# Relative-bias attention and a snake feed-forward layer on one core: the order of the opening's loads, zero products and bias factors

## The chip, the cores and the metric

One core of one Trainium2 chip. The metric is device time of one execution in microseconds (us). Engines are called PE (TensorE, matrix products), ACT (ScalarE), DVE (VectorE), POOL (GpSimd) and SP (SyncE, which only issues transfers here).

## The reference

Attention over 8 batch entries with 8 heads, 576 positions and 64 columns a head, with a bias that depends on the distance of two positions alone; its output, 4608 rows by 512, goes through a feed-forward layer of width 2048.

```python
scores = scale * np.matmul(q, k.transpose(0, 1, 3, 2))      # scale = 1/8
bucket = ...                                                # of |i - j|, 31 from 116 on
scores = scores + bias_table[bucket].transpose(2, 0, 1)[None]
attn = softmax(scores)
x = np.matmul(attn, v)                                      # -> (8*576, 512)
h = x @ w_in                                                # 512 -> 2048
s = np.sin(alpha * h)
g = h + s * s / (alpha + 1e-09)
out = g @ w_out                                             # 2048 -> 512, float32
```

## The kernel before

Everything is computed in fp16 with fp32 sums. For each batch entry t the kernel makes transposed scores (keys on the 128 partitions, queries along the row), takes their exponential on ACT, multiplies the band near the diagonal by a factor exp(bias - last bias) on DVE, and multiplies by the values with a column of ones beside them, which gives the softmax's sum as well. DVE divides by it (`norm_av`), PE or a transfer turns the result into `xT`, and then come the products with `w_in` (16 blocks f of 128 columns), sine, square, `g`, and the products with `w_out`. After the opening PE works through all this without a gap.

**Planner.** The order of instructions on each engine comes from a list scheduler in the kernel (`Plan`). A task has costs for the engines that may run it, dependencies, a priority `pri` (lower first) and a time `nb` before which it isn't taken. The planner always takes the task with the earliest start; among those within 0.02 us on one engine, the one with the lowest `pri`. The plan's clock is its own; what the engines then do is in that order, and each waits for its operands. A "fill" is a product of zeros (`warm1`) of 192 columns that is put on PE where the plan would leave it free for over `WARM_GAP`, from plan time `WARM_FROM` to `WARM_END`; a task's `pad` lists further zero products that always follow it if a bank of the accumulator is free. A fill holds a bank in the planner's books.

**Opening, t = 0.** SP loads k and then q of heads 0 and 1 (`nat0`), then the values of heads 0 and 1 (`load_v32`, fp32, cast later by POOL). ACT's queue loads the bias table, the constant `phi`, and alpha. POOL loads heads 2 to 5 (`load_pair`), later 6 and 7. DVE casts k, DVE and POOL each one half of q. PE turns k and q of a pair of heads p (`plan_tr`: PE transposes, a copy on DVE, for k also `tail` on POOL, which puts the last 64 keys into `kts`). The bias: PE subtracts the last bucket (`less`), ACT takes exp into `tabE`, PE multiplies it by `phi` (8 partitions x 512), ACT copies that to `e_sb` and writes it in several copies to the scratch tensor `e_dram`; SP waits for that write and then reads from it, with one element's shift for each partition, the band rows `m2r` (heads 0-1, 2-3, 4-7) and `mhr`, rows for the last 64 keys. Behind them SP loads the values of heads 4 to 7.

The scores of t = 0 run unit by unit (`plan_att0`): for each pair p four units "A" of 128 keys (two products of 512 columns, one for each head) and one unit "C" for the last 64 keys. Each unit: PE, then exp on ACT (L704), then the factor product `bd` on DVE (L735 for A; for C L721, on DVE for p = 0 and on POOL for the others). POOL's first load of `w_in` stands behind a one-element copy `tick` from `m2r`, so that it waits for the last band rows; behind it come the loads of k, q of t = 1 and `w_out` (`loads2`) and the values of t = 1 (`loads3`). `clear` sets the zeros and ones in the second set of buffers, which t = 1 needs.

Constants that the change touches: `T_FIRST` (k's and q's first transposes), `T_TAB` (`less`), `T_PAIR` (transposes of pairs 1 to 3), `T_M2`, `T_MH` (factor products), `T_V0`, `T_VA`, `T_VB` (values' loads and casts), `T_WI`, `T_CL`, `T_W`, `T_TR1`, `T_WO` (w_in's loads, clear, first products with w_in, transposes of t = 1, first products with w_out). `T_ACT` lists pairs whose q copy goes to ACT.

Of the kernel before, what the change touches and what calls it, by code (L numbers as in the profile page):

```python
# [10 lines left out]
F16 = mybir.dt.float16  # L11
# [50 lines left out]
class Plan:  # L62
# [86 lines left out]
    def run(self, t0):  # L149
        free = {e: t0 for e in ("PE", "ACT", "DVE", "POOL", "SP")}  # L150
        todo = list(self.tasks)
        while todo:
# [33 lines left out]
            if e == "PE" and WARM_FROM < free[e] < WARM_END and st > free[e] + WARM_GAP:  # L186
                if self.fill(free[e], 192):
                    free[e] += 0.083
                    continue
# [27 lines left out]
PRI_S = 0  # L217
T_WI = 16.8
T_TAB = 5.2
T_CL = 24.5  # L220
T_FIRST = (4.75, 5.95)
T_PAIR = ((7.9, 8.5), (9.3, 10.2), (11.6, 12.3))
T_ACT = ()
T_M2 = (13.0, 14.8, 16.0, 16.0)
T_MH = 14.2
T_RST = 25.0
T_V0 = (5.8, 6.4, 8.9, 9.6)
T_P3 = 7.0
T_VA = (10.5, 11.0)
T_VB = (19.5, 19.5, 19.5, 19.5)  # L230
T_AL = (10.0, 560)
# [7 lines left out]
T_V = ((15.5, 19.0), (50.0, 50.0))  # L239
T_TR1 = (36.0, 39.0)  # L240
T_W = (25.5, 30.5)
T_WO = (40.5, 43.0, 45.7, 48.3)
WARM0 = 8
WARM1 = 2
WARM_LAG = 0.3
WARM_GAP = 0.12
WARM_FROM = 7.3
AV_PRI = 400
# [18 lines left out]
def kernel(  # L267
# [25 lines left out]
    EW = 512  # L293
    NE = 5

# [6 lines left out]
    staged_q = nc.dram_tensor("staged_q", [T, S, H * D], F16, kind="Internal")  # L302
    e_dram = nc.dram_tensor("e_dram", [NE, 4 * H, EW], F16, kind="Internal")

# [76 lines left out]
    def bank(b, n=1):  # L381
        k = b.banks[0]
        return pb[:, k, :] if n == 1 else pb[:, k : k + n, :]
# [31 lines left out]
    def load_v32(h):  # L415
        nc.sync.dma_start(out=vst[:, h], in_=v[0, h, 0:512].rearrange("(c p) d -> p c d", p=128))
# [36 lines left out]
    def full(out, lhsT, rhs, start, stop):  # L453
        nc.tensor.matmul(out=out, lhsT=lhsT, rhs=rhs, start=start, stop=stop)  # L454
# [13 lines left out]
    def load_m2r(eng, h0, h1, r):  # L468

        eng.dma_start(  # L470
            out=m2r[:, h0:h1],
            in_=bass.AP(tensor=e_dram, offset=EW * (4 * H * r + h0), ap=[[1, 128], [EW, h1 - h0], [1, XW]]),
        )

    def load_mhr(eng):
        for z in range(2):
            eng.dma_start(
                out=mhr[64 * z : 64 * z + 64],
                in_=bass.AP(tensor=e_dram, offset=EW * (4 * H * (1 + z) + z) + 192,
                            ap=[[1, 64], [2 * EW, NP], [1, 192]]),  # L480
            )
# [31 lines left out]
    P_.tensor_copy(out=natb[:, 1, :, 1], in_=x0[:, :, 1])  # L513

# [5 lines left out]
    def loads3():  # L520
        load_v16(1)
# [16 lines left out]
    def plan_tr(t, p, kq, pri, nb, deps=()):  # L538
# [45 lines left out]
    def plan_table():  # L584

        a, b = Buf("h"), Buf("h")

        def less(e):
            full(bank(a)[0:NB, 0:H], less_last, tabN, True, True)

        def ex(e):
            nc.scalar.activation(out=tabE, in_=bank(a)[0:NB, 0:H], func=AF.Exp)

        x = plan.add({"PE": 0.06}, less, [], -1200, nb=T_TAB, new=[a])
        x.pad = (256,)
        x = plan.add({"ACT": 0.12}, ex, [x], -1200, use=[a])

        def mm(e):
            full(bank(b)[0:H, 0:EW], tabE, phi_sb, True, True)

        def cp(e):
            nc.scalar.activation(out=e_sb, in_=bank(b)[0:H, 0:EW], func=AF.Copy)
# [52 lines left out]
    def plan_unit(t, p, kind, c, u, ub, done, gate, base):  # L655
# [51 lines left out]
        x = plan.add({"ACT": n / 1200.0 + 0.065}, ex, [mark] + gate, base + 20, use=[b, ub])  # L707
        late = 0.0 if t else T_MH if kind == "C" else T_M2[p]
        if kind == "X":
# [6 lines left out]
        elif kind == "C":  # L716
            ys = slice(0, 2) if two else slice(y, y + 1)

            def bd(e):
                io = u.v[:, ys, 8, 384:512]  # L720
                k_of(e).tensor_tensor(  # L721
                    out=io, in0=io, in1=mh[:, 2 * g + ys.start : 2 * g + ys.stop, 0:128], op=ALU.mult
                )
# [38 lines left out]
    def plan_att0(g, gates, gate):  # L762
# [6 lines left out]
        for i, unit in enumerate(runs):  # L769
# [5 lines left out]
            def run(e, i=i, x=x):  # L775
# [6 lines left out]
                if g == 1 and i == len(runs) - 1:  # L782
# [444 lines left out]
```

## Time and profile before

| | us |
|---|---|
| three runs | 375.42, 375.47, 377.07 |
| median | 375.47 |
| profiled execution, device time | 376.99 |
| its span in the profile | 375.1 |
| PE busy in the span | 367.5 (98%) |
| ACT, DVE, POOL busy | 309.7, 262.3, 92.7 |
| first score product / first exp | 7.91 / 8.45 |
| `e_dram` write issued / SP's first `m2r` load issued | 6.90 / 10.75 |
| first factor product on DVE | 16.17 |
| `tick` on POOL / first `w_in` load issued | 20.18 / 20.69 |
| last exp of t = 0 ends | 28.5 |
| first product with `w_in` | 30.44 |

Times below the fourth row count from the start of the span. Busy times of PE are those of pipelined products, so 98% isn't 98% of its peak. Between the span and the device time lie 1.9 us.

### The profile page before, as it was taken

How to read it: one execution, taken by the hardware profiler on the slowest of the kernel's cores; microseconds unless marked ns; L12 is line 12 of the kernel's file. 1: busy time of each engine (PE TensorE's matmuls, PEld its weight loads, DVE VectorE, ACT ScalarE, POOL GpSimd, SP SyncE). 2: the span in 40 equal slices, each digit the busy share in tenths (PEclk: the TensorE clock that was granted, in tenths of full speed). 3: DMA queues.
4: the chain of work that ended last, by engine and by line, in shares of the span. 5: the costliest groups of instructions: out<-in, count | busy, mean ns of one | idle time of the engine just before them, and what ended most of it. 6: DMA issues, size and time to landing. Idle time of an engine off the chain costs nothing.

```text
span 375.1 us, 8928 instructions
## 1 busy us (share of the span) xinstructions
PE 367.5 (98%) x3576; PEld 196.4 (52%) x3576; DVE 262.3 (70%) x569; ACT 309.7 (83%) x421; POOL 92.7 (25%) x133
## 2 busy tenths in 40 slices
PE   7989999999999999999999999999999999999996
PEld 3465545644464445784564456444666456444443
DVE  3696976778676957696769767886769576879000
ACT  3797989889997979797979799879979797999211
POOL 7477360064000910064004600190006000000000
PEclk9799999999999999999999999999999999999999
DMA  9979999599724992299929992799259121000112
GB/s 167 190 139 206 199 167 147 120 98 122 123 61 97 103 174 73 68 144 137 130 54 140 118 163 58 133 92 172 69 97 121 65 57 48 7 27 5 72 69 85
DMA packets 149114, 40.49 MB, mean 108 GB/s; under 512 B 137080, under 2 KB 143568, under 8 KB 149072
## 3 DMA queue, kind: packets, MB, share of 16 engines
q0 software_dynamic: 96032, 17.67, 58.2%
q1 hardware_dynamic: 52864, 22.16, 24.2%
q8 instruction: 28, 0.46, 0.5%
q10 hardware_dynamic: 176, 0.09, 0.1%
q14 instruction: 14, 0.11, 0.1%
HBM read 37.73 MB, written 16.56 MB: 145 GB/s over the span
## 4 chain that ended last, share of the span: by engine, by line
PE 93%; ACT 4%; DMA 1%; DVE 0%; issue 0%; POOL 0%; SPq 0%; ACTq 0%
PE pb L454 91%; ACT u L704 4%; PE pb L553 1%; DMA natx<-in_q_dram 1%; PE pb L1021 1%; DVE qT L536 0%; POOL natx L513 0%; PE pb L547 0%; DVE xn L950 0%; DVE u L735 0%; SPq L429 0%; ACT outs L534 0%; ACT xT L534 0%; PE pb L643 0%; PE pb L931 0%
## 5 line engine op out<-in xcount | busy, mean ns | idle before, releaser
L704 ACT ACTIVATE u<-pb 128x1024 f16<-128x1024 f32 (+1 forms) x146 | 136.1, 1019 | 18.2 <-PE pb L454 18.0
L454 PE MATMUL pb<-w_out,g 128*128 128x512 f16 (+2 forms) x592 | 138.6, 374 | 0.0
L454 PE MATMUL pb<-xT,w_in 128*128 128x512 f16 (+4 forms) x704 | 127.6, 340 | 0.0
L1079 DVE SCALAR_TENSOR_TENSOR g<-sq,inv_a,pb 128x512 f16<-128x512 f16 x144 | 101.1, 744 | 6.8 <-ACT sq L1072 2.8
L1065 ACT ACTIVATE s<-pb,alphaT 128x512 f16<-128x512 f32 x144 | 92.9, 693 | 14.2 <-PE pb L454 13.2
L454 PEld LDWEIGHTS <-w_in 128*128 128x128 f16 x704 | 64.5, 98 | 57.2
L454 PEld LDWEIGHTS <-g 128*128 128x128 f16 x592 | 53.5, 98 | 63.0 <-issue 9.1
L735 DVE TENSOR_TENSOR u<-u,m2r 128x512 f16<-128x512 f16 (+1 forms) x128 | 61.6, 492 | 25.1 <-ACT u L704 24.1
L454 PEld LDWEIGHTS <-u 128*128 128x128 f16 x1152 | 43.8, 97 | 8.0 <-issue 2.3
L399 POOL COPY kt<-kT 64x256 f16<-64x256 f16 x12 | 5.1, 422 | 173.7 <-DMA kT<-staged_k 173.4
L454 PE MATMUL pb<-qT,kT 64*128 64x64 f16 (+1 forms) x512 | 45.1, 289 | 1.9 <-ACT u L704 1.0
L454 PE MATMUL pb<-v,u 128*128 128x65 f16 x1024 | 43.7, 193 | 0.0
L1072 ACT ACTIVATE sq<-s 128x512 f16<-128x512 f16 x65 | 41.1, 640 | 1.2 <-DVE g L1079 0.3
L1074 DVE TENSOR_TENSOR sq<-s 128x512 f16<-128x512 f16 x79 | 32.7, 423 | 12.6 <-ACT s L1065 11.5
L950 DVE TENSOR_TENSOR xn<-pb,rd 128x256 f16<-128x256 f32 (+2 forms) x59 | 28.5, 483 | 2.0
L454 PEld LDWEIGHTS <-kT 64*128 64x128 f16 x512 | 16.4, 94 | 24.2 <-issue 16.9
L454 PE MATMUL pb<-vh,u 128*128 128x130 f16 x128 | 28.2, 220 | 0.0
L404 POOL DMA_DIRECT2D v<-in_v_dram x28 | 24.8, 895 | 4.2 <-DMA nat<-in_q_dram 2.1
L949 DVE RECIPROCAL rd<-pb 128x4 f32<-128x4 f32 (+2 forms) x59 | 11.1, 188 | 19.6 <-PE pb L454 18.7
L534 ACT ACTIVATE outs<-pb 128x512 f32<-128x512 f32 (+2 forms) x11 | 6.2, 568 | 19.9 <-PE pb L454 19.9
L536 DVE COPY outs<-pb 128x512 f32<-128x512 f32 x26 | 17.9, 687 | 2.9 <-PE pb L454 2.7
L1143 ACT ACT_TABLE_LOAD x15 | 19.2, 1283 | 0.3
(75 smaller groups left out, 188.3 us busy)
## 6 DMA issues: line engine op xcount, KB each, us to landing
out_dram<-outs SPq DMA_DIRECT2D x35, 256.0 KB, 2.3
v<-in_v_dram POOLq DMA_DIRECT2D x28, 128.0 KB, 4.3
staged_k<-in_k_dram POOLq DMA_DIRECT2D x6, 576.0 KB, 8.9
staged_q<-in_q_dram POOLq DMA_DIRECT2D x6, 576.0 KB, 12.5
w_in<-in_moe_w_in_dram POOLq DMA_DIRECT2D x4, 512.0 KB, 8.9
w_out<-in_moe_w_out_dram POOLq DMA_DIRECT2D x4, 512.0 KB, 14.9
w_out<-in_v_dram SPq DMA_DIRECT2D x6, 128.0 KB, 6.8
xT<-xn SPq DMA_TRANSPOSE x47, 2.4
```

The lines of the kernel that those rows point to most:

```text
L404: nc.gpsimd.dma_start(out=vs[t % 2][:, c, :, 0:D], in_=vp[128 * c : 128 * c + 128],)
L454: nc.tensor.matmul(out=out, lhsT=lhsT, rhs=rhs, start=start, stop=stop)
L536: k_of(e).tensor_copy(out=o, in_=i)
L704: nc.scalar.activation(out=o, in_=x, func=AF.Exp, scale=0.125)
L735: nc.vector.tensor_tensor(out=io, in0=io, in1=m2[:, 2 * p : 2 * p + 2, x0 : x0 + hi - lo], op=ALU.mult)
L949: nc.vector.reciprocal(out=r, in_=x[:, :, :, D])
L950: nc.vector.tensor_tensor(out=xn[:, 0:n].rearrange("p c (z d) -> p c z d", z=2), in0=x[:, :, :, 0:D], in1=r.unsqueeze(3).to_broadcast([128 ...
L1065: nc.scalar.activation(out=s16.v, in_=h.v, func=AF.Sin, scale=alphaT[:, f : f + 1])
L1072: nc.scalar.activation(out=sq.v, in_=s16.v, func=AF.Square)
L1074: k_of(e).tensor_tensor(out=sq.v, in0=s16.v, in1=s16.v, op=ALU.mult)
L1079: nc.vector.scalar_tensor_tensor(out=gcell[b].v[:, f, :], in0=sq.v, scalar=inv_a[:, f : f + 1], in1=h.v, op0=ALU.mult, op1=ALU.add,)
L1143: nc.scalar.preload_act_table_set(name)
```

## The change

- q's cast goes whole to DVE (POOL did half). Values of heads 0 to 3 are loaded by SP, behind a one-element `memset` on DVE that follows k's cast (before: heads 0 and 1 directly behind q on SP, heads 2 and 3 by POOL with `load_vh`).
- `tabE` has its 8 columns twice, so that the table's product fills 16 partitions; it is written to `e_dram` from 16 partitions in two copies each (before: 8 partitions, five copies each). The band rows come in four loads of two heads, each from its own copy.
- `mhr` isn't loaded. For t = 0 unit C multiplies by the band rows themselves, in two halves of 64 partitions; for later t `make_mhr` on POOL copies `mhr` out of `m2r`.
- Zero products: none after `less`, two after the table's product, one after k's first transposes (before two), none after q's (before three); all others 320 columns for 256. `WARM_FROM` 6.3 for 7.3; a fill before plan time 8.2 costs 0.163 in the plan.
- The copy of pair 3's q goes to ACT. Due times: most are earlier by 0.4 to 2.5, `T_CL` is later by 6.

```diff
             if e == "PE" and WARM_FROM < free[e] < WARM_END and st > free[e] + WARM_GAP:
                 if self.fill(free[e], 192):
-                    free[e] += 0.083
+                    free[e] += 0.083 if free[e] > WARM_COLD else 0.163
...
-T_WI = 16.8
-T_TAB = 5.2
-T_CL = 24.5
-T_FIRST = (4.75, 5.95)
-T_PAIR = ((7.9, 8.5), (9.3, 10.2), (11.6, 12.3))
-T_ACT = ()
-T_M2 = (13.0, 14.8, 16.0, 16.0)
-T_MH = 14.2
+T_WI = 15.8
+T_TAB = 5.3
+T_CL = 30.5
+T_FIRST = (4.75, 5.45)
+T_PAIR = ((7.5, 8.2), (8.8, 9.7), (11.4, 12.1))
+T_ACT = (3,)
+T_M2 = (12.2, 13.4, 14.6, 15.6)
-T_V0 = (5.8, 6.4, 8.9, 9.6)
+T_V0 = (5.0, 5.7)
-T_VA = (10.5, 11.0)
-T_VB = (19.5, 19.5, 19.5, 19.5)
+T_VA = (9.6, 10.0, 10.6, 11.2)
+T_VB = (18.5, 18.5, 18.5, 18.5)
-T_TR1 = (36.0, 39.0)
-T_W = (25.5, 30.5)
-T_WO = (40.5, 43.0, 45.7, 48.3)
+T_TR1 = (33.5, 37.0)
+T_W = (24.5, 29.5)
+T_WO = (39.0, 41.6, 44.2, 46.8)
+PAD = 320
-WARM_FROM = 7.3
+WARM_FROM = 6.3
+WARM_COLD = 8.2
...
-    NE = 5
+    NE = 4
-    e_dram = nc.dram_tensor("e_dram", [NE, 4 * H, EW], F16, kind="Internal")
+    e_dram = nc.dram_tensor("e_dram", [NE // 2, 2 * H, 4, EW], F16, kind="Internal")
-    tabE = sgl.tile([NB, H], F16, name="tabE")
+    tabE = sgl.tile([NB, 2 * H], F16, name="tabE")
-    e_sb = sgl.tile([H, EW], F16, name="e_sb")
+    e_sb = sgl.tile([2 * H, EW], F16, name="e_sb")
...
     def load_m2r(eng, h0, h1, r):
+        j, m = r // 2, H * (r % 2) + h0
...
-    def load_mhr(eng):
+    def make_mhr():
         for z in range(2):
-            eng.dma_start(...)
+            r = slice(64 * z, 64 * z + 64)
+            P_.tensor_copy(
+                out=mhr[r], in_=m2r[r, z::2, 192 - 64 * z : 384 - 64 * z]
             )
...
-    load_v32(0)
-    load_v32(1)
...
     cast0(0, nc.vector)
-    x0 = nat0[:, 1].rearrange("s two (i d) -> s i two d", i=SI)
-    nc.vector.tensor_copy(out=natb[:, 1, :, 0], in_=x0[:, :, 0])
-    P_.tensor_copy(out=natb[:, 1, :, 1], in_=x0[:, :, 1])
+    nc.vector.memset(vst[0:1, 0:4, 0, 0:1], 0.0)
+    for h in range(4):
+        load_v32(h)
+    cast0(1, nc.vector)
...
-            m.pad = (256,) if p else (192,) * (2, 3)[kq]
+            m.pad = (PAD,) if p else (192,) * (1, 0)[kq]
...
-            nc.scalar.activation(out=tabE, in_=bank(a)[0:NB, 0:H], func=AF.Exp)
+            nc.scalar.activation(
+                out=tabE.rearrange("b (r h) -> b r h", r=2),
+                in_=bank(a)[0:NB, 0:H].unsqueeze(1).to_broadcast([NB, 2, H]), func=AF.Exp,
+            )
-        x.pad = (256,)
...
             nc.scalar.dma_start(
-                out=e_dram.ap()[:, 0:H].rearrange("r h x -> h r x"),
-                in_=e_sb.unsqueeze(1).to_broadcast([H, NE, EW]),
+                out=e_dram.ap()[:, :, 0].rearrange("j m x -> m j x"),
+                in_=e_sb.unsqueeze(1).to_broadcast([2 * H, NE // 2, EW]),
             )
-            load_m2r(nc.sync, 0, 2, 0)
-            load_mhr(nc.sync)
-            load_m2r(nc.sync, 2, 4, 3)
-            load_m2r(nc.sync, 4, H, 4)
+            for r in range(4):
+                load_m2r(nc.sync, 2 * r, 2 * r + 2, r)
...
         x = plan.add({"PE": 0.25}, mm, [x], -1100, new=[b])
+        x.pad = (192,) * 2
...
+            plan.add({"POOL": 0.7}, lambda e, i=i: load_vt(0, i), [], 9000 + i, nb=T_V0[i])
+        for i in range(4):
             plan.add({"POOL": 0.45}, lambda e, i=i: cast_v(i), [], 9004 + i, nb=T_VA[i])
-        for i in range(4):
-            plan.add({"POOL": 0.7}, lambda e, i=i: load_vt(0, i) if i < 2 else load_vh(0, i),
-                     [], 9000 + i, nb=T_V0[i])
...
-            P_.tensor_copy(out=tick, in_=m2r[0:1, 4, 0:1])
+            P_.tensor_copy(out=tick, in_=m2r[0:1, 6, 0:1])
...
+        plan.add({"POOL": 2.5}, lambda e: make_mhr(), [], 9006, nb=T_CL + 1.0)
...
-        late = 0.0 if t else T_MH if kind == "C" else T_M2[p]
+        late = 0.0 if t else T_M2[p]
...
+                for z in range(2):
+                    r = slice(64 * z, 64 * z + 64)
+                    io = u.v[r, y, 8, 384:512]
+                    k_of(e).tensor_tensor(
+                        out=io, in0=io, in1=m2[r, 2 * p + z, 64 * z : 64 * z + 128], op=ALU.mult
+                    )
-            d = plan.add({"POOL": 0.45} if t == 0 and p else {"DVE": 0.25 if two else 0.15}, bd, [x],
+            d = plan.add({"POOL": 0.6} if t == 0 and p else {"DVE": 0.25 if two else 0.3}, bd, [x],
                          base + 10, nb=late, use=[ub])
...
-            m.pad = (256,)
+            m.pad = (PAD,)
```

More of the change, by code (lines that the diff above doesn't have):

```diff
@@ L468, in load_m2r @@
     def load_m2r(eng, h0, h1, r):
+        j, m = r // 2, H * (r % 2) + h0
         eng.dma_start(
             out=m2r[:, h0:h1],
-            in_=bass.AP(tensor=e_dram, offset=EW * (4 * H * r + h0), ap=[[1, 128], [EW, h1 - h0], [1, XW]]),
+            in_=bass.AP(tensor=e_dram, offset=4 * EW * (2 * H * j + m),
+                        ap=[[1, 128], [4 * EW, h1 - h0], [1, XW]]),
         )
-    def load_mhr(eng):
+    def make_mhr():
         for z in range(2):
[L477 to L480, printed above, removed]
+            r = slice(64 * z, 64 * z + 64)
+            P_.tensor_copy(
+                out=mhr[r], in_=m2r[r, z::2, 192 - 64 * z : 384 - 64 * z]
             )
@@ L591, in ex @@
         def ex(e):
-            nc.scalar.activation(out=tabE, in_=bank(a)[0:NB, 0:H], func=AF.Exp)
+            nc.scalar.activation(
+                out=tabE.rearrange("b (r h) -> b r h", r=2),
+                in_=bank(a)[0:NB, 0:H].unsqueeze(1).to_broadcast([NB, 2, H]), func=AF.Exp,
+            )
         x = plan.add({"PE": 0.06}, less, [], -1200, nb=T_TAB, new=[a])
-        x.pad = (256,)
         x = plan.add({"ACT": 0.12}, ex, [x], -1200, use=[a])
         def mm(e):
-            full(bank(b)[0:H, 0:EW], tabE, phi_sb, True, True)
+            full(bank(b)[0 : 2 * H, 0:EW], tabE, phi_sb, True, True)
         def cp(e):
-            nc.scalar.activation(out=e_sb, in_=bank(b)[0:H, 0:EW], func=AF.Copy)
+            nc.scalar.activation(out=e_sb, in_=bank(b)[0 : 2 * H, 0:EW], func=AF.Copy)
             nc.scalar.dma_start(
-                out=e_dram.ap()[:, 0:H].rearrange("r h x -> h r x"),
-                in_=e_sb.unsqueeze(1).to_broadcast([H, NE, EW]),
-            )
-            load_m2r(nc.sync, 0, 2, 0)
-            load_mhr(nc.sync)
-            load_m2r(nc.sync, 2, 4, 3)
-            load_m2r(nc.sync, 4, H, 4)
+                out=e_dram.ap()[:, :, 0].rearrange("j m x -> m j x"),
+                in_=e_sb.unsqueeze(1).to_broadcast([2 * H, NE // 2, EW]),
+            )
+            for r in range(4):
+                load_m2r(nc.sync, 2 * r, 2 * r + 2, r)
             for h in range(4, H):
@@ L716, in plan_unit @@
         elif kind == "C":
-            ys = slice(0, 2) if two else slice(y, y + 1)
             def bd(e):
[L720 to L723, printed above, removed]
-            d = plan.add({"POOL": 0.45} if t == 0 and p else {"DVE": 0.25 if two else 0.15}, bd, [x],
+                if two:
+                    io = u.v[:, :, 8, 384:512]
+                    nc.vector.tensor_tensor(out=io, in0=io, in1=mh[:, p : p + 2, 0:128], op=ALU.mult)
+                    return
+                for z in range(2):
[5 more added lines that the diff above has]
+            d = plan.add({"POOL": 0.6} if t == 0 and p else {"DVE": 0.25 if two else 0.3}, bd, [x],
                          base + 10, nb=late, use=[ub])
```

## The prediction

> **What bounds the kernel now.** I read the chain of waits in order of time first, because it says where the opening ends and what ends it.
>
> ```profile
> 7.10 0.77 DVE qT L536
> 7.91 0.82 PE pb L454 x3
> 8.73 0.62 PE pb L553 x6
> ...
> 14.74 11.19 ACT u L704 x13
> ...
> 28.56 0.43 DVE u L735
> ...
> 32.01 7.34 PE pb L454 x34
> ```
>
> From 29.60 on the chain is TensorE alone. So whatever the change does before about 30 us counts only by how much sooner TensorE's unbroken work starts. Before that the chain goes by TensorE (7.91 to 14.72), then ScalarE's exponentials (14.74 to 28.5), then one factor product, a normalisation and a turn. Next the busy times by stretch (columns: length, then busy time and count of PE, PEld, DVE, ACT, POOL, then granted clock, DMA share, GB/s):
>
> ```profile
> 4.65:8.07 3.42, 2.40 (x26) 1.42 (x24) 1.94 (x4) 0.75 (x2) 2.12 (x5) 1.00 1.28 199
> 8.07:11.48 3.41, 3.41 (x34) 1.58 (x32) 1.03 (x2) 2.05 (x2) 3.33 (x7) 0.50 1.22 151
> 11.48:14.89 3.41, 3.41 (x25) 1.39 (x24) 1.85 (x5) 1.77 (x3) 1.26 (x5) 0.50 1.18 171
> 8.45:14.74 6.29, 6.29 (x54) 2.87 (x53) 2.75 (x6) 3.67 (x4) 4.21 (x10) 0.50 1.21 159
> 14.74:28.53 13.79, 12.59 (x207) 8.38 (x205) 12.68 (x34) 13.79 (x17) 8.11 (x18) 0.99 0.82 168
> 16.17:30.08 13.91, 11.99 (x207) 8.37 (x205) 13.33 (x38) 13.80 (x18) 9.53 (x22) 1.00 0.86 172
> 30.40:371.80 341.40, 341.28 (x3264) 181.45 (x3261) 241.70 (x513) 288.30 (x394) 72.53 (x85) 1.00 0.83 103
> ```
>
> Three facts. The clock is half from 8.07 to 14.89, and ScalarE idles 6.29 - 3.67 = 2.62 us there because TensorE feeds it slowly. From 14.74 ScalarE has no gap. From 16.17, the first factor product, VectorE is nearly full as well (13.33 of 13.91). So two chains end within half a microsecond of each other, and both must get shorter. After 30.40 TensorE idles 0.12 us in 341: nothing is to be had there.
>
> The timeline and the waits say what sets the start of each (start, length, then idle before):
>
> ```profile
> 5.89 0.69 POOL L513 CAST natx<-natx 96x384 f16<-96x384 f32 x1 [1.52 <-DMA natx<-in_q_dram]
> 10.75 0.37 SPq L470 DMA_DIRECT2D m2r<-e_dram  x1
> 11.16 1.33 SPq L477 DMA_DIRECT2D mhr<-e_dram  x2
> 16.17 0.41 DVE L735 TENSOR_TENSOR u<-u,m2r 128x512 f16<-128x512 f16 x1
> SPq L470 <- DMA e_dram<-e_sb: 7.9, 1, 7.9
> ```
>
> The queries' cast on GpSimd ends at 6.58; SP stands until the table is in DRAM at 10.75; the band rows' first load lands 4.3 us later (shortest of its group) at 15.05.
>
> **Queries first.** Before, q's load took 4.6 us from issue, k's, alone in front, 3.4 (the DMA issues). Bounds for q without the two values' loads behind it: 1.28 + 3.4 = 4.7 to the 5.83 of now. The values' loads stand behind q, not ahead, so I take 5.5. The whole cast on VectorE costs the 0.56 of k's (L464) for GpSimd's 0.69. The queries' transposes start at 6.1 (6.63 before). But k's copy (0.75), which started at 6.13, now stands behind that cast on VectorE; then q's copy (0.76) at 6.85, first scores at 7.65 for 7.91: **-0.3**. The small memset on VectorE (row of its like 0.06) falls in idle time before q lands.
>
> **Table.** In TensorE's queue its product now stands behind the queries' transposes: 5.87 becomes 6.5, so its copy and its write start 0.6 later. The write took 10.75 - 6.90 = 3.85; other small loads took 2.7 (bias table, 1 KB) and 3.9 (phi, 36 KB). From 7.5 that lands between 10.2 and 11.4; I take 10.9, near phi's. The Trainium skill (DMA: Bandwidth & Descriptors, "How many engines (k)") says 16 partitions spread a transfer over 16 engines and 8 over 8. That would make it five rows an engine before and two after, an estimate of 3.2 us and a landing at 10.7; no view here shows the spread.
>
> **Band rows.** Two loads of mhr (1.33 us on SP, 192 KB) and two values' loads on GpSimd's queue no longer compete, but four values' loads (128 KB each) now stand ahead on SP's queue, issued from 4.9. Bounds for the first load: 3.4 (k's, alone) to 5.4 (the median of the two); I take 4.0, near the 4.3 of now. First rows: 14.9 (13.6 to 16.8), 15.05 before. The other three follow without mhr between; the last landed at 20.1 and should at about 17.5.
>
> **VectorE's chain.** From the first factor product it had 13.9 us of work. The last queries' copy goes to ScalarE (-0.76), pair 0's last-key product becomes two halves (+0.2, one row 0.21): 13.3, some 0.4 less if a copy comes to stand ahead of it. 14.9 + 12.9..13.3 = 27.8 to 28.2, against 30.08.
>
> **ScalarE's chain.** It takes 0.65 more for that copy. By the planner's rules, worked by hand with the new constants: k's transposes 4.75, q's 5.45, table 5.86 to 6.11, first scores 7.03. TensorE's planned free time, 6.11, lies under the new WARM_FROM of 6.3, so no filler goes into the gap; the early zeros' products are 1 + 2 = 3 (six before: 2 + 1 + 3). After the second score run bank 6 holds a filler until 8.56, so the third run (8.43) goes ahead of pair 1's queries. That feeds ScalarE one exponential sooner, but the last of pair 0's runs still has three transposes before it. Each filler grows by 64 columns, 0.05 us at half clock, seven of them 0.37 (0 if the clock is full). If the clock stays half to 14.89 the chain is -0.3 + 0.37 - 0.3 (one filler fewer) + 0.65 = +0.4. If it is full one stretch sooner, three score runs, two transposes (0.69 to 0.45 each) and fillers (0.39 to 0.28) lose some 1.3: -0.9.
>
> **The rest.** w_in: GpSimd's dummy copy waited for the last band rows until 20.18; at 17.5 all of w_in is some 2.7 sooner. Its second part landed by the rows at about 29.5 (8.9 from issue), just ahead of the first product at 30.44, so without this the gain would stop at 0.9; with it, the cover holds. The weights behind it on GpSimd's queue come as much sooner, which no unbroken TensorE needs. Last-key products on GpSimd become two halves, each between 0.24 (a 64x64 copy) and 0.62: up to +0.6 for each of three, beside 1.35 of idle time; if that cover is gone, the last one costs 0.6. The mhr copies and the clears go to GpSimd after 30 and are needed at 48: nothing. GpSimd's four casts of values stand ahead of the keys' copies for pairs 1 and 2: if the loads land after 12, those wait, with several us to spare.
>
> **The sum.** The profiled execution took 376.99 (span 375.1 and 1.9 around it), the median of the runs is 375.47 and one of three is 377.07; so the 2.62 us of idle ScalarE may be partly missing from the median run. There VectorE's chain, 13.9 less about half a us of copies from rows at 15.05, ends near 28.5, which fits the 1.5 us. Against that the change gives 27.8 to 28.2, less what GpSimd's halves may cost: -0.3 to -0.7; on the profiled course ScalarE's -0.9 binds: 376.1. Bounds of the rows and of q add 1.3 to the gain, or 1.9 to the loss. I take -0.9 on the median, between the two with the first scores' 0.3: **374.6**.
>
> **Rivals.**
> *Half clock stays.* 3.42 us with TensorE 70% busy (2.40) lost the clock. In the next stretch the transposes took 1.38 of 3.41 and the clock did not return; in the one after 0.69, and it returned. The new order has two transposes in that stretch again, and fewer early products: the opening does not do what its words say. ScalarE's +0.4 on the profiled course, nothing on the median: 375.8. For: three products in place of six. Against: longer fillers, third scores ahead. The Trainium skill (TensorE: Matmul & The Clock Gate, Part 1 and Part 4) says the clock is judged in free-running windows of about 3.4 us and that transposes do not count as busy. The trace agrees, 8.07 to 14.89 being two times 3.41; by it this rival comes true wherever the windows fall as here.
> *Values in the way (slower).* Four values' loads are not through when the band rows are issued at 10.9 behind them. Before, four such loads took SP 5.31 us from 13.70 to issue alone. If the first rows land at 17.7 instead of 14.9, VectorE ends at 31.0, 0.9 past the profile's 30.08 and 2.4 past the median's 28.5: 377.8. It decides from 16.8 on. Against: two of them, issued from 1.76, landed by about 9 (6.8 us is the median), and the change issues its four from 4.9.
> *Full clock throughout (faster).* If 7.65 comes before the clock drops, ScalarE needs 20.08 - 2.62 + 0.65 = 18.1 from 8.2, to 26.3, and with rows at 13.6 VectorE ends at 26.5 to 26.9: 3.4 less than the profile, 373.4. For: the short gaps; a free row of SP. Against: 13.6 is the bound, not the middle.
>
> **How the numbers follow.** About 0.5% (1.9 us) is what a measurement of this kernel can tell from no change. Forecast 0.36 (of it 0.03 past -0.5%), half clock 0.15 (0.01 past +0.5%), values in the way 0.15, full clock 0.34. So faster 0.37, within 0.47, slower 0.16. The range goes from 372.7, below the full clock's case by the bound of q (0.7), to 377.0, the top of the forecast and of the half clock's case; the slower rival is left outside. The forecast's own range is 373.6 to 375.6.
>
> **What would show it.** Right: first score matmul near 7.6, first factor product near 14.9, the dummy copy near 17.5, no score run behind pair 1's queries until the third; TensorE's unbroken stretch from about 28.5. Granted clock by stretch decides between the rivals. I am wrong if the first factor product stands after 16, if VectorE has gaps after it, or if w_in's products wait for w_in.

## The result: 378.48 us for 375.57, and the profile after

| | before | after |
|---|---|---|
| median of five runs, us | 375.57 | 378.48 (378.26 to 379.28) |
| ratio | | 1.0073, 95% interval 1.0051 to 1.0095 |
| profiled execution / its span | 376.99 / 375.1 | 378.77 / 376.8 |
| first score product / first exp | 7.91 / 8.45 | 7.50 / 7.94 |
| table's write issued / SP's first `m2r` load issued | 6.90 / 10.75 | 7.56 / 12.94 |
| first factor product on VectorE | 16.17 | 16.60 |
| `tick` on GpSimd / first `w_in` load issued | 20.18 / 20.69 | 21.61 / 21.90 |
| last first-pass exp ends / first product with `w_in` | 28.5 / 30.44 | 30.7 / 31.33 |

The change made the kernel slower by 2.9 us, against a forecast of 0.9 faster. The chain of waits of after has two new links near its front (columns: start, length, what):

```profile
6.95 0.59 ACT e_sb L604
7.56 5.36 DMA e_dram<-e_sb
12.94 3.56 DMA m2r<-e_dram
16.60 1.36 DVE u L741 x3
...
33.06 19.25 DMA w_out<-in_moe_w_out_dram
52.35 4.46 PE pb L455 x54
```

Before, the chain went by TensorE and ScalarE from 7.91 to 28.5; no transfer but q's load was on it. Now it takes in the table's round trip through DRAM: 5.36 us to write it (3.85 before), 3.56 to read the first rows. The timeline gives the pieces (start, length, engine and line, then idle time before and who ended it):

```profile
5.56 0.56 DVE L465 CAST natx<-natx 96x768 f16<-96x768 f32 x1 [0.79 <-DMA natx<-in_q_dram]
7.50 0.39 PE L455 MATMUL pb<-qT,kT 64*128 64x512 f16 x2 [0.32 <-DVE qT L536]
4.82 2.66 SPq L417 DMA_DIRECT2D w_out<-in_v_dram  x4
7.56 0.33 ACTq L605 DMA_DIRECT2D e_dram<-e_sb  x1
12.94 1.91 SPq L471 DMA_DIRECT2D m2r<-e_dram  x4
16.60 1.36 DVE L741 TENSOR_TENSOR u<-u,m2r 128x512 f16<-128x512 f16 x3 [0.63 <-DMA m2r<-e_dram]
17.88 0.75 DVE L536 COPY qT<-pb 128x576 f16<-128x576 f16 x1
18.69 0.61 PE L455 MATMUL pb<-qT,kT 64*128 64x512 f16 x2 [0.52 <-DVE qT L536]
21.61 0.35 POOL L630 COPY tick<-m2r 1x1 f16<-1x1 f16 x1 [0.79 <-DMA m2r<-e_dram]
```

Read in pairs. The queries came as forecast (first two lines). The four values' loads are issued from 4.82 to 7.48, and the table's write directly behind them, at 7.56; SP reaches its first row load at 12.94. The last rows land at 21.6, 7.2 us after their issue. VectorE stands at its first factor product until 16.60 with a copy of queries queued behind it, and TensorE waits 0.5 us for that copy. By stretch (length; busy time and count of PE, PEld, DVE, ACT, POOL; granted clock; DMA share; GB/s):

```profile
8.07:11.48 3.41, 3.41 (x44) 1.73 (x43) 1.45 (x2) 2.85 (x3) 1.35 (x4) 0.61 1.41 213
11.48:14.89 3.41, 3.41 (x30) 1.34 (x28) 1.43 (x5) 2.08 (x3) 1.62 (x5) 0.50 0.34 67
14.89:18.30 3.41, 3.28 (x39) 1.57 (x35) 2.45 (x5) 2.61 (x5) 0.46 (x2) 0.50 0.61 120
31.30:373.10 341.80, 341.50 (x3264) 181.61 (x3262) 241.66 (x513) 289.37 (x396) 74.28 (x93) 1.00 0.83 103
```

From 11.48 to 14.89 the transfer engines moved 67 GB/s where the kernel before moved 171: they waited for the table. From 14.89 on they read rows at 120 GB/s. After 31.30 TensorE is busy 341.5 of 341.8 us, so it has no long wait there, as before.

The opening isn't quite all of the loss. The last copy out of the accumulator stands in the two chains at (before, after):

```profile
371.88 0.28 ACT outs L534
373.12 0.28 ACT outs L534
```

Between these two executions the first product with `w_in` comes 0.9 later, this last copy 1.2, and the end of the span 1.6 (375.14 and 376.77). From the start of the copy to the end of the span SyncE waits for the last stores to land: 3.26 us before, 3.65 after, where the last store landed 1.99 us from its issue for 1.60. So 0.4 us of the loss lie at the end of the program.

Nor are the clocks alike. The half clock lasted 13.65 us in this execution; the other four had a mean clock of 0.990 or 0.991, about half as much half clock, and took 378.26 to 379.28, so the longer stretch doesn't show in the time. But none of the five kept the full clock, and most executions of the kernel before did, by their mean clock. Where it didn't, it took 376.99 and 377.07 at a mean of 0.991, and 378.57 and 378.64 at 0.982, where the profiled execution of after took 378.77. So at 0.991 the change costs some 1.4 of the 2.9 us, and at 0.982, on three executions, next to nothing. How much of the loss came by the lost clock, and whether the longer waits lost it, no run of the whole change separates.

### The profile page after: what moved, and what is told of

Same layout as the page of the kernel before. It is cut to its first block, busy times and chain, and to the rows that moved or that the text cites. A ratio compares the mean times of both kernels' runs of the same rounds, so it can differ in the third digit from the quotient of the medians.

```text
span 376.8 us, 8920 instructions
## 1 busy us (share of the span) xinstructions
PE 369.6 (98%) x3568; PEld 197.0 (52%) x3568; DVE 261.7 (69%) x569; ACT 311.0 (83%) x423; POOL 94.2 (25%) x137
## 4 chain that ended last, share of the span: by engine, by line
PE 87%; DMA 9%; POOL 1%; ACT 1%; DVE 1%; issue 0%; SPq 0%; ACTq 0%; DVEq 0%
PE pb L455 86%; DMA w_out<-in_moe_w_out_dram 5%; DMA e_dram<-e_sb 1%; DMA natx<-in_q_dram 1%; DMA m2r<-e_dram 1%; ACT u L705 1%; POOL w_out L441 1%; POOL nat L430 0%; PE pb L1027 0%; DVE u L741 0%; POOL u L727 0%; DVE qT L536 0%; ACT e_sb L604 0%; DVE natx L465 0%; PE pb L547 0%
## 5 line engine op out<-in xcount | busy, mean ns | idle before, releaser
L705 ACT ACTIVATE u<-pb 128x1024 f16<-128x1024 f32 (+1 forms) x146 | 136.6, 1016 | 18.1 <-PE pb L455 17.9
L455 PEld LDWEIGHTS <-u 128*128 128x128 f16 x1152 | 44.6, 98 | 9.1 <-issue 2.2
L455 PE MATMUL pb<-qT,kT 64*128 64x64 f16 (+1 forms) x512 | 45.9, 294 | 1.0 <-DVE qT L536 0.8
L455 PE MATMUL pb<-v,u 128*128 128x65 f16 x1024 | 44.9, 194 | 0.3 <-DVE u L741 0.2
L956 DVE TENSOR_TENSOR xn<-pb,rd 128x256 f16<-128x256 f32 (+2 forms) x59 | 28.5, 483 | 2.0
```

Source lines behind the costliest of these rows:

```text
L705: nc.scalar.activation(out=o, in_=x, func=AF.Exp, scale=0.125)
L956: nc.vector.tensor_tensor(out=xn[:, 0:n].rearrange("p c (z d) -> p c z d", z=2), in0=x[:, :, :, 0:D], in1=r.unsqueeze(3).to_broadcast([128 ...
```

## The experiments

Each kernel is timed beside the kernel before, whose median was 375.38 to 375.40 in four of the five groups and 375.75 in the last (5 KB rows, due times on after).

### The values' loads, added to before and taken from after

```diff
 # on before: heads 0 to 3 on SP behind a memset, none by GpSimd
-    load_v32(0); load_v32(1)
+    nc.vector.memset(vst[0:1, 0:4, 0, 0:1], 0.0)
+    for h in range(4): load_v32(h)
...
 # GpSimd then casts four heads for two; on after: the reverse
```

> The kernel before with the values' part alone: heads 0 to 3 by SP behind the memset after k's cast, no values' loads by GpSimd; q's cast still half on each engine. Theory 'table late': the table's write lands at 12 to 13 instead of 10.7, the band rows 1.3 to 2 later, and the kernel is 0.7 to 1.8 us slower: 376.1 to 377.2. Rival (the values' loads are harmless where VectorE has other work until 16): 375.4 within 0.4.

Measured: 377.66 (377.0 to 378.02), ratio 1.0051, 1.0031 to 1.007: this part alone costs the kernel before 2.3 us. It is slower than the executions of before beside it at like mean clock too: 377.35 to 378.02 for 376.09 to 377.02 at 0.994 and 0.995, and 377.0 to 378.02 for 374.73 to 376.05 from 0.998 on. Its timeline:

```profile
4.84 2.05 SPq L416 DMA_DIRECT2D w_out<-in_v_dram  x4
6.88 0.53 ACTq L604 DMA_DIRECT2D e_dram<-e_sb  x1
12.37 0.37 SPq L470 DMA_DIRECT2D m2r<-e_dram  x1
```

The write is issued as early as before (6.88 for 6.90) and takes 5.49 us to SP's next step in place of 3.85 (3.05 to 3.63 in the other traces of before and its variants whose table is written from 8 partitions with no values ahead). The values hold up the table's write, on another queue, before they could hold up any row.

> The changed kernel with the values' loads as before: heads 0 and 1 on SP directly behind q, heads 2 and 3 by GpSimd; no memset. Theory 'table late' (four values' loads from 4.82 stand ahead of the table's write in the transfers, which lands at 12.94 instead of 10.75, so the band rows, the dummy copy and w_in come late): the write lands before 11.5, SP's first m2r issue is before 11.6, the dummy copy before 20.5, and 1.5 to 3 us of the 2.9 us lost come back: 375.5 to 377.0. Rival 'halves' (GpSimd's last-key products of 1.07 to 1.36 us for 0.43 to 0.76): the m2r issue moves but the time stays above 377.8. Rival 'half clock': time follows the half-clock stretch, 13.65 us in the profile, and not the m2r issue.

Measured: 376.73 (375.74 to 377.62), ratio 1.0017, 0.9989 to 1.0045: 1.75 under after, and each of its twelve runs is under each of after's. What is left is seen in its timeline:

```profile
10.49 1.91 SPq L471 DMA_DIRECT2D m2r<-e_dram  x4
16.94 1.36 DVE L740 TENSOR_TENSOR u<-u,m2r 128x512 f16<-128x512 f16 x3 [3.48 <-DMA m2r<-e_dram]
18.22 0.75 DVE L535 COPY qT<-pb 128x576 f16<-128x576 f16 x1
19.03 0.61 PE L455 MATMUL pb<-qT,kT 64*128 64x512 f16 x2 [4.07 <-DVE qT L535]
```

The rows are issued at 10.49, 2.45 sooner than in after, and yet the first product comes at 16.94: the first load took 6.35 us. VectorE stands 3.48 us for it, the copy of queries stands behind, and TensorE idles 4.07. Two more costs show here: the rows' own reading, and VectorE's order. The profiled execution was the slowest of the twelve (377.62), and its last copy out of the accumulator starts at 373.08, as in after. The 0.9 us between the two spans lie behind that copy (2.81 us for 3.65), so this trace doesn't show where in the opening the rest of the 1.75 was won.

### The spacing of the table's rows

After puts the rows of two heads 4 KB apart in DRAM (`[NE // 2, 2 * H, 4, EW]`, a row is 1 KB); in the kernel before they are 1 KB apart.

```diff
 # on before: s = 2, 3, 4, 5 in four kernels (with s = 5 also 5 * H * r); on after the reverse (s = 1)
-offset=EW * (4 * H * r + h0), ap=[[1, 128], [EW, h1 - h0], [1, XW]]
+offset=EW * (4 * H * r + s * h0), ap=[[1, 128], [s * EW, h1 - h0], [1, XW]]
 # mhr's rows and the write likewise
```

> The kernel before with the table's rows 4 KB apart in DRAM and nothing else changed. Theory 'row spacing': the last band rows land at 21.5 or later instead of 20.1 and the kernel is 0.5 to 2 us slower: 376 to 377.5. If spacing does nothing: 375.4 within 0.4.

Measured: 380.80 (380.26 to 381.11), ratio 1.0132, 1.0108 to 1.0156. Spacing alone costs the kernel before 5.4 us.

> The changed kernel with the table's rows 1 KB apart in DRAM instead of 4 KB (the unused three slots of each row left out); everything else as in the changed kernel. Theory 'row spacing' (the band rows come slowly because rows that are 4 KB apart are read at some 155 packets in a us, where the kernel before read up to 300): the four band-row loads land within 4 us of the first one's issue instead of 8.6 (12.94 to 21.56), the dummy copy stands before 19, and 1 to 2 us comes back: 376.5 to 377.5. Rival 'table late' alone: the loads need as long as now, and the time is 378.5 within 0.4.

Measured: 377.67 (376.86 to 380.7), ratio 1.0067, 1.0045 to 1.0089: 0.8 under after by the medians, but the two intervals overlap, so by the times alone the part isn't clear of noise in after. The traces show it. The transfers of 14.9 to 17.9 us (queue: packets, MB, share of 16 engines' time), first of after, then of this kernel:

```profile
q1 hardware_dynamic: 497, 0.36, 63.8%
```

```profile
q1 hardware_dynamic: 1353, 0.74, 95.3%
```

That is 3.0 x 16 x 0.638 / 497 = 62 ns a packet with 4 KB. With 1 KB it is 34, but there 562 of the packets are shorter than 512 bytes, in after 26. Packets of 512 bytes and more came at 157 a us with 4 KB and 264 with 1 KB. From the issue of the first rows to the landing of the last it took 8.1 to 8.6 us in four kernels with 4 KB rows behind the values (after among them), and 6.7 to 7.5 in four of the change's kernels with 1 KB. The kernel before pays more for 4 KB; a likely reason is that it also reads `mhr` from these rows and its last load has four heads. `tick` came at 24.14 there for 20.18, in after at 21.61 for 19.94.

> The kernel before with the table's rows in DRAM 2 KB apart in place of 1 KB, nothing else (4 KB took 380.80). Theory A, the cost lies in strides of a large power of two (rows that share a low address): 2 KB costs part of it, 376.5 to 379, and 3 KB none. Theory B, the cost grows with the distance: 2 KB costs a third of 5.4, 376.5 to 377.5, and 3 KB two thirds. Theory C, only from 4 KB on: 375.2 to 375.8.

> The kernel before with the table's rows 3 KB apart in place of 1 KB, nothing else. Theory A, a matter of powers of two: 375.2 to 376. Theory B, a matter of distance (rows that lie further apart are fetched at a lower rate): 378 to 380.

> The kernel before with the table's rows in DRAM 5 KB apart in place of 1 KB, nothing else (2 KB took 376.16, 3 KB 375.79, 4 KB 380.80, beside 375.39). Theory A, the cost comes with the power of two that the rows' addresses share: 375.2 to 376.2, and the band rows' packets as short as in the kernel before. Theory C, it comes with any distance of 4 KB or more: 380 to 382.

Measured: 2 KB 376.16 (ratio 1.0018, 0.9995 to 1.0041), 3 KB 375.79 (1.0019, 0.9989 to 1.0049), 5 KB 376.40 (1.0016, 0.9986 to 1.0047). All three intervals hold 1. So it isn't distance: 5 KB costs nothing that can be told, 4 KB costs 1.3%. Whether 2 KB costs a little stays open. The transfers of 12.9 to 15.9 us, first of before, then with 4 KB, then with 5 KB:

```profile
q1 hardware_dynamic: 951, 0.49, 68.6%
```

```profile
q1 hardware_dynamic: 537, 0.24, 69.3%
```

```profile
q1 hardware_dynamic: 938, 0.49, 87.4%
```

At the same share of engine time, little over half as many packets went through: 3.0 x 16 x 0.686 / 951 = 35 ns a packet (41 in a second profile of before), 3.0 x 16 x 0.693 / 537 = 62 ns with 4 KB, 45 ns with 5 KB. Engines look equally busy in the first two; only the packet count and the bytes tell that a packet takes longer on average. It isn't every packet: those of the 768-byte rows took 36 ns in the median in both, 47 and 110 ns in the mean. The time from issue to landing of the row loads, with 4 KB:

```profile
DMA to landing us min/median/max: 5.9/8.5/11.0
```

In the kernel before it was 4.3, 6.5 and 6.9.

### Both taken out of after

After with both reverse edits, the values' and the rows' (s = 1).

> The changed kernel with both: values' loads as before and rows 1 KB apart. If 'table late' and 'row spacing' are both causes and add, the first band rows land before 14 and all before 16.5, VectorE has no long stop ahead of the first factor product, and the time is 374.0 to 375.5, at or below the kernel before. If row spacing does nothing: 376.7 within 0.4, as with the values alone.

Measured: 375.84 (374.93 to 376.87), ratio 1.0007, 0.9992 to 1.0021. The medians add up (1.75 + 0.81 = 2.56, measured 2.64), as far as the 0.81 can be trusted. By the profiles 0.8 us of the 2.64 lie at the end of the program again (2.80 us from the last copy to the end of the span, 3.65 in after). First rows landed at 14.54, the last at 18.21. The loss is gone, and so is the gain: the time is that of before.

This profile needs care. Its mean clock is given as 1.00, but the record of the clock begins only at 17.3, and two products of scores took (start, length):

```profile
13.74 0.61 PE L455 MATMUL pb<-qT,kT 64*128 64x512 f16 x2
17.37 0.39 PE L455 MATMUL pb<-qT,kT 64*128 64x512 f16 x2
```

The opening ran as slowly as in the half-clock stretch of after (0.61 at 16.39 there). A mean of 1.00 therefore doesn't prove that an execution kept the clock. VectorE waited for TensorE's transposes here, and the first factor product stood at 16.87, long after its rows.

### VectorE's order

```diff
-T_M2 = (12.2, 13.4, 14.6, 15.6)
+T_M2 = (13.0, 14.8, 16.0, 16.0)      # as before
```

This puts the copy of the second pair's queries ahead of the first factor products on VectorE, and one more product by zeros on TensorE.

> The kernel after with values' loads and row spacing as before (375.84), and the due times of the factor products as before (13.0, 14.8, 16.0, 16.0 in place of 12.2, 13.4, 14.6, 15.6), which puts the copy of the second pair's queries ahead of the first factor products on VectorE; the order of the rest is the same but for one product by zeros more. Theory A, TensorE's wait for that copy behind the first factor products (0.5 us at 18.2 in the profile of after) is what keeps the pair from beating the kernel before: 374.8 to 375.3. Theory B, TensorE has slack there, and the due times change nothing: 375.6 to 376.1.

Measured, on the kernel with both parts taken out: 374.69 (373.97 to 377.08), ratio 0.9984, 0.9957 to 1.0011. 7 of its 12 runs lie under the fastest without the edit (374.93). Its timeline:

```profile
14.62 1.02 DVE L740 TENSOR_TENSOR u<-u,m2r 128x768 f16<-128x768 f16 x2
18.34 0.46 POOL L629 COPY tick<-m2r 1x1 f16<-1x1 f16 x1 [1.02 <-DMA m2r<-e_dram]
```

The first product starts at 14.28 and VectorE stands for rows only 0.4 us there; the granted clock was 1.00 and the first product with `w_in` came at 27.69. The medians put this version 0.7 under before and 3.8 under after; that it beats before isn't certain, since the interval reaches 1.0011. Nor is it shown that the copy's place is the cause. The seven fast ones ran at a mean clock of 0.999 or 1.00 (373.97 to 374.80), four at 0.986 to 0.995 took 375.92 to 377.08, one at 1.00 took 377.06, and the profile without the edit ran its opening at half clock. So the clock, which the added product by zeros might also touch, is a rival that no run settles.

> The kernel after, whole, with only the factor products' due times as before (the copy of the second pair's queries ahead of the first factor products on VectorE). On the repaired kernel this edit was worth 1.15 us (375.84 to 374.69). Theory A, the three costs add: 377.1 to 377.6. Theory B, while the rows land at 16.5 to 21.6 the copy's place is hidden behind the later rows, and the edit is worth under 0.4: 378.0 to 378.6.

Measured, on after whole: 377.98 (377.29 to 378.95), ratio 1.0067, 1.005 to 1.0085, 0.5 under after: between the two theories, and its range overlaps that of after (378.26 to 379.28), so the size of this part is not settled. The rows landed late as before the edit (`tick` at 20.6), and most of the loss stayed.

### Parts that were not the cause

**16 partitions for the table's write.**

```diff
 # on after
-in_=e_sb.unsqueeze(1).to_broadcast([2 * H, NE // 2, EW])
+in_=e_sb[0:H].unsqueeze(1).to_broadcast([H, NE, EW])
 # on before: tabE and e_sb doubled as in the change, NE = 6
-in_=e_sb.unsqueeze(1).to_broadcast([H, NE, EW])
+in_=e_sb.unsqueeze(1).to_broadcast([2 * H, NE // 2, EW])
```

> The changed kernel with the table written from 8 partitions, four copies each, at the same places in DRAM; the product still makes 16 rows. Theory 'table late' with the last of 16 transfer engines as its end: the write lands 0.5 to 1.3 us earlier than at 12.94, and 0.3 to 1 us comes back: 377.5 to 378.2. If the number of partitions is not what delays it: 378.5 within 0.3, or later. Rival 'halves': no change, 378.5.

Measured, 8 partitions with four copies in after: 378.11 (377.06 to 378.99), ratio 1.0057, 1.0028 to 1.0085, no worse than 16; its write took 4.67 us to SP's next step.

> The kernel before with one part of the change: the table is computed twice over and written from 16 partitions, three row pairs of 8 KB each give six copies of it (before: five copies from 8 partitions), rows 1 KB apart as before. Theory A, the write from 16 partitions lands 1 us sooner (2.8 us from its issue to the first rows' issue, against 3.85) and the first factor product follows: 374.4 to 375.0, w_in's first load issued near 19.7 against 20.69. Theory B, the rows' own packets at 14 to 20 us set when the rows land, and the earlier write changes nothing: 375.2 to 375.6.

Measured, 16 partitions with three copies in before: 375.62 (374.84 to 379.03), ratio 1.0004, 0.998 to 1.0028. Its write took 3.95 us to land, against 3.05 to 3.85 to SP's next step from 8 partitions with five copies. With 16 partitions, two copies and no values ahead it took 2.8 to 3.5. The part is worth nothing that shows.

**The last keys' factors.**

```diff
-            for r in range(4): load_m2r(nc.sync, 2 * r, 2 * r + 2, r)
+            load_m2r(nc.sync, 0, 2, 0); load_mhr(nc.sync)
+            for r in range(1, 4): load_m2r(nc.sync, 2 * r, 2 * r + 2, r)
 # and whole products from mhr, no copies on GpSimd
```

> The changed kernel with mhr loaded by SP behind the first band rows as before, the last-key products whole, and no mhr copies on GpSimd. Rival 'halves': GpSimd's products fall to 0.43 to 0.76 and 0.5 to 1.5 us comes back, 377.0 to 378.0, although the later band rows land 1 us later still. Theory 'table late': the later band rows and the dummy copy move from 21.6 to 22.5 or so, and the time is 378.5 to 379.5.

Measured, on after: 380.56 (380.45 to 381.01), ratio 1.0125, 1.0083 to 1.0166. `mhr` was read from the 4 KB rows there, and `tick` waited until 24.1, so I tried it again on the kernel with both parts taken out.

> The kernel after with the same two parts as before, and the last keys' factors loaded in one transfer of their own as before (two DMAs behind the first rows on SP's queue, whole last-key products of 128 partitions, no copies for them on GpSimd). Theory A, the halved products on GpSimd (1.1 to 1.4 us each in the profile of after, where before's took 0.4 to 0.8) are on the chain from the last first-pass exps to the first w_in product: 375.0 to 375.4, 0.4 to 0.8 under the pair's 375.84. Theory B, they stand beside idle time and the two added DMAs push the last rows back by some 1.5 us on SP's queue, as the trial with 4 KB rows did: 376.2 to 377.3.

Measured: 377.50 (376.13 to 377.99), ratio 1.0036, 1.0011 to 1.0062, so 1.7 above the same kernel with halves. Of the last-key products on GpSimd (ns: min/median/max), first after, then this kernel:

```profile
L727 POOL TENSOR_TENSOR u<-u,m2r x6: 415/609/657, 19.5 to 28.9; 64x128 f16<-64x128 f16 x6
```

```profile
L726 POOL TENSOR_TENSOR u<-u,mhr x3: 428/429/467, 16.5 to 26.2; 128x128 f16<-128x128 f16 x3
```

A half costs at least as much as a whole, so a pair took 1.07 to 1.36 us where it took 0.43 to 0.76 before. Yet with whole products and the two loads back the kernel is slower, so going back to them is no gain. What whole products would be worth without the loads isn't shown. The profiled execution of this kernel was one of its three fastest (376.26), so where the 1.7 us lie in the others isn't shown.

**All planned times, and the zeros.**

```diff
 # after; the first group alone in the second kernel, which has the values and rows as before
-m.pad = (PAD,) if p else (192,) * (1, 0)[kq]
+m.pad = (256,) if p else (192,) * (2, 3)[kq]
+x.pad = (256,)                        # behind less; none behind the table's product
-WARM_FROM = 6.3; WARM_COLD = 8.2
+WARM_FROM = 7.3; WARM_COLD = 0.0
 # all of them
-T_WI, T_TAB, T_CL, T_FIRST, T_PAIR, T_ACT, T_M2, T_VB, T_TR1, T_W, T_WO of after
+the same of before
```

> The changed kernel with all planner constants, pads and the last queries' copy as before (T_WI, T_TAB, T_CL, T_FIRST, T_PAIR, T_ACT, T_M2, T_VB, T_TR1, T_W, T_WO, WARM_FROM, pads of 256 and 2, 1, 3 of 192); transfers and products as in the changed kernel. Theory 'table late': the table's product is ahead of the queries' transposes again, its write is issued at about 6.9 instead of 7.56, and lands 0.3 to 0.7 earlier; 0.3 to 1 us comes back, 377.5 to 378.2. Rival 'half clock' (the plan's fewer early zeros cost the clock): the half-clock stretch falls to 6.8 us or less and most of the loss comes back, 375.5 to 377.

Measured, after with every constant of the plan as before: 379.73 (378.51 to 381.01), ratio 1.0101, 1.0057 to 1.0146, 1.25 above after. Its waits of TensorE from 45 to 60 us (total, times, longest):

```profile
PE pb L455 <- DMA w_out<-in_moe_w_out_dram: 1.5, 1, 1.5
```

With `T_CL` as before, the clears and the `mhr` copies stand ahead of `w_out`'s loads on GpSimd, which are issued from 34.05 on for 30.83, and TensorE waits 1.5 us for them. After puts them behind, and there TensorE takes up the last part just as it lands (the chain of waits, 52.35).

> The kernel after with two parts as before (the four values' loads back where they were, table rows 1 KB apart; that pair gave 375.84 beside a before of 375.39) and a third: the products by zeros ahead of and behind the table are as before (two and three on the first two key transposes, one of 256 on the table's, none behind it, pads of 256 later). Theory A, the changed zeros cost the clock that the kernel before keeps in most executions: 375.1 to 375.5, the clock at 1.00 in most runs, 0.3 to 0.7 under the pair. Theory B, the clock is not what separates them and what is left lies in the halves of the last keys and in the order behind 16 us: 375.6 to 376.1, as the pair.

Measured: 377.00 (374.92 to 377.65), ratio 1.0024, 0.9999 to 1.0049, and a mean clock of 0.990 to 0.995 in all 12 executions. So putting the early zeros back doesn't bring the clock back, and the theory that their loss cost it isn't borne out. With the zeros of the change five of 12 are given as 1.00, but one of these is the profile above that ran its opening at half clock, so how often that kernel kept it isn't known.

**The queries, and a second look at before.**

```diff
...
-nc.vector.tensor_copy(out=natb[:, 1, :, 0], in_=x0[:, :, 0])
-P_.tensor_copy(out=natb[:, 1, :, 1], in_=x0[:, :, 1])
+cast0(1, nc.vector)
```

> The kernel before with the query part alone: both halves of q cast by VectorE in one instruction (before, half by GpSimd), the order of all else as before. Theory A, first scores 0.3 us sooner carry through ScalarE's exps to the end: 374.9 to 375.2. Theory B, what ends the first pass is when the band rows land and the last first-pass products follow, so sooner scores only lengthen a wait: 375.2 to 375.6, first factor product still near 16.2.

Measured: 375.58 (374.8 to 378.91), ratio 1.0015, 0.9987 to 1.0042: q's cast on VectorE alone is worth nothing that shows. Its waits, 12 to 22 us:

```profile
DVE u L733 <- DMA m2r<-e_dram: 1.7, 1, 1.7
```

VectorE waits for the rows, so a sooner score lengthens that wait.

> The kernel before, unchanged, for a profile of one of its usual executions. Expected: 375.0 to 375.6, the granted clock at 1.00 all through, against 0.991 and 376.99 in the profile shown first. If the half clock cost the rest, the first w_in product comes 0.8 to 1.6 us before 30.44; if it stays at 30.4 the half clock was beside other waits.

Measured: median 375.67 (374.79 to 377.07). The profiled execution again took 377.07 with the clock at half from 8.13 to 14.96, the same course as the first profile; five of the eight runs had a mean of 1.00 and took 374.79 to 375.96. The profile shown first is thus not the usual course. In the kernel with q's cast alone, whose profiled execution (375.52) kept the clock, the first factor product stands at 14.96 and the first product with `w_in` at 29.10, not at 16.17 and 30.44. Set against that course, after's first product with `w_in` is 2.2 us later, not 0.9.

## Why the prediction was wrong, step by step

- **Queries first**: right. q landed at 5.54 (5.5), first scores at 7.50 (7.65). That this carries to the end was wrong: alone it gave nothing that shows.
- **Table**: the step that failed first. It took the nearest rows of small loads, 2.7 and 3.9, though none of these had four loads of 128 KB ahead; 12.94 instead of 10.9. Without the values ahead, the rows were issued at 10.49: the step's size was right for a kernel that the change wasn't.
- **Rivals, Values in the way**: it had the mechanism and the price (2.4; the values alone cost before 2.3), but put it on the rows, and took as its point of decision first rows at 16.8; the first rows landed at 16.50 and it was slower all the same. The argument against, that two loads from 1.76 had landed by 9, weighed them against the rows at 10.9, and overlooked that the table's write is issued at 7.56, 0.1 us behind the fourth.
- **Band rows**: the first load took 3.6 us (4.0 forecast), but the last landed at 21.56 for 17.5. 2.0 of it came with the table. For the other 2 us the sum had no term: the spacing of 4 KB, which stands in the new shape of `e_dram` in the change's diff and which no step of the prediction mentions. With 1 KB the last rows landed 1.8 us sooner (19.75). With both taken out, rows landed at 14.54 and 18.21, near the forecast's 14.9 and 17.5.
- **VectorE's chain**: its 12.9 to 13.3 us from the first product would have ended at 29.9; the first pass ended on ScalarE at 30.67 and GpSimd's last half ended at 29.28. "Some 0.4 less if a copy comes to stand ahead of it" saw only one side: the second pair's copy of queries stood behind the factor products, and TensorE waited for it (0.5 us); what that cost in time is not settled.
- **ScalarE's chain** and *Half clock stays*: the order was as worked by hand (third score run ahead of pair 1's queries, three early products by zeros), and the clock stayed at half for even longer in the profile, 13.65 us. The rival gave this 375.8 and nothing on the median. At a mean clock of 0.991 after was still 1.4 us slower than before, so it isn't the whole; its share is open. The Trainium skill (TensorE: Matmul & The Clock Gate, Part 1) has windows of about 3.4 us; the 13.65 us are four times 3.41, which agrees. *Full clock throughout* didn't come: the clock was 0.61 from 8.07 to 11.48.
- **The rest**: `w_in` was 1.2 us later, not 2.7 sooner, as `tick` waited for the last rows. The halves on GpSimd, up to +0.6 each by the forecast, took 0.4 to 0.7 more each.
- **The sum**: it chose -0.9 on the median from a profile of the less usual course. With the values, the spacing and VectorE's order put right, the kernel came to 374.69, near the 374.6 of the sum; its interval goes from 373.8 to 375.8 (0.9957 and 1.0011 of 375.39), so this shows no more than that the other terms were not far off together. Part of that nearness is luck: 0.45 of its 0.7 us under before lie at the end of the program (2.81 us for 3.26 from the last copy on), which the sum didn't have.
- The Trainium skill's rule of 16 partitions for 16 engines (DMA: Bandwidth & Descriptors, "How many engines (k)") gave an estimate of 3.2 us for the write. Runs gave 2.8 to 3.5 with two copies and no values ahead, 5.36 with them: its estimate lies in the first range, and what other queues had issued outweighed it. A gain by the spread itself isn't shown, since 8 partitions took 3.05 to 3.85.

## What to carry to other kernels

When a small transfer starts a chain (write, wait, read back), look at what all queues have issued in the 3 us before it, not only at its own queue; moving a bulky load "out of the way" of one transfer can put it in front of a more urgent one. Check the address strides of every layout that a change touches, also where they look like bookkeeping. An engine's due times belong to the arrival times they were set for: move one without the other and a wait for data can turn into a wait for whatever is queued behind it. Before a profile is compared with another, look at what clock each ran at in its opening, and at what follows the last product.

## What was not expected of the hardware

Reading overlapping rows from DRAM that lie 4 KB apart took 62 ns a packet where 1 KB took 35 to 41 and 5 KB took 45, and cost 5.4 us in a kernel of 375; 2, 3 and 5 KB cost nothing that can be told. Of the five distances only the multiple of 4 KB is slow; no other multiple was tried, and why it is slow isn't shown. The second surprise is the clock: the same kernel before had a mean clock of 1.00 in most executions and lost two stretches of 3.41 us in others, both profiled ones among them, at times some 1.5 us longer (377.07 for a median of 375.67).
